# Attention and MoE in one planned stream on one core: a pair's transposes and the next pair's scores taken together, both on half rows of TensorE

## The chip, the cores and the metric

One core of a Trainium2 chip runs the program once. The metric is the device time in microseconds; the figures "before" are three executions, and the profile is of a fourth execution, taken by the hardware profiler. TensorE is written PE here, its weight loads PEld, VectorE DVE, ScalarE ACT, GpSimd POOL, the DMA-issuing engine SP.

## The reference

For 4 batches, 8 heads, 768 positions and 64 values a head, attention looks at the first 8 positions and at the last 96, with a distance bias; its output, 3072 rows of 512 values, goes through a two-matrix MLP with an ELU between:

```python
scores = scale * np.matmul(q, k.transpose(0, 1, 3, 2)) + bias
scores = np.where(is_global | is_local, scores, -1e9)
a = softmax(scores); attn = np.matmul(a, v)
x = attn.transpose(0, 2, 1, 3).reshape(3072, 512)
h = x @ w_in                                  # 512 -> 2048
g = np.where(h > 0, h, np.exp(np.minimum(h, 0)) - 1)
return g @ w_out                              # 2048 -> 512
```

All values are float32. The kernel reaches that precision on TensorE in two ways: with plain f32 operands, or by splitting an operand into a high part of type f32r and a low part that is the rest, and adding the products high x high, low x high and high x low.

## The kernel before, in words

The 3072 rows are cut into 12 groups of 256 rows (4 batches x 3 places in the sequence); a group is two row tiles of 128. The heads are taken in 4 pairs, so a group has 4 pairs of attention and then 16 chunks of the MLP (`moe`, chunks `fc`), each of 12 `h` matmuls of 256 columns (L631) and 6 `o` matmuls of 512 columns (L661). The attention of a group runs while the MLP of the group before it runs, on the same engines.

Nothing in the program text is the order of execution. Every piece of work is added to a `Plan` with its engine and a guessed duration, what it reads and writes, and a due time. `Plan.order` then goes through all of it as a list scheduler: an engine takes, of the pieces whose inputs are ready by the guessed times, the one with the earliest due time. `slack` adds to the time at which inputs from another engine count as ready (`SLACK` 600 ns, `BEHIND` 1200 ns). The order so found is the order in which each engine's instructions are emitted, and on the chip each engine takes them in just that order. Buffers are named slots (`SLOTS`): the PSUM banks are `s0`, `s1` (scores), `t0` (transposes), `v0` (output of attention), `h0`, `h1`, `o0`, `o1` (MLP).

Groups 0 to 3 take attention in plain f32 (`pair32`): there the two heads of a pair lie in partitions 0 to 63 and 64 to 127, and their score matmuls (L532) use 64 rows of the PE array each, with outputs in two banks. From the fifth group on (n = 4 to 11, 32 pairs, 8 of them at the start of a sequence, where the first row tile has 128 keys instead of 232) `pair` and `head` do this for a pair:

- load queries, values and keys (L419, L420) into the single buffers `rqv0` and `rk0`; queries and keys come twice, so that each head has all 128 partitions;
- split queries into `qd` (L445) and `ql` (L450), and keys into `ks` whose upper 64 partitions hold the low part (L287, L295); one matmul of 128 rows then gives two of the three products, and a second with `ql` the third;
- per head and row tile: two score matmuls of 232 columns (L585), the bias and row maximum on DVE (L493), the exponential on ACT (L495); per head one inverse of the sums (L508, L509); per row tile the normalisation on DVE (L481), two transposes on PE of 116 keys each (L599), high part on ACT (L287) and low part on DVE (L295) of the transposed weights, and two matmuls with the values (L611), 256 columns each;
- add the two halves of the output (L287, L472) and split it for the MLP (`xh`, `xl`).

So PE visits attention about twelve times for a pair, with two to four instructions each, and does MLP work between. `build` sets the due times: the pairs of group n are spread evenly over the time from the MLP start of group n-1 to 4000 ns before the MLP start of group n (`LEAD`).

## Time and profile before

| what | us |
|---|---|
| three executions, median (lowest to highest) | 708.03 (706.6 to 709.02) |
| the profiled execution | 704.46 |
| its span, first to last instruction | 702.7 |
| PE busy in the span | 688.3 (98%) |
| PEld / DVE / ACT / POOL busy | 613.1 / 497.7 / 495.1 / 227.0 |
| mean granted clock of PE, share of full | 0.997 |

Busy time of PE counts matmuls from start to a modelled end; matmuls overlap, so a matmul's duration in the trace (283 ns for an `h` matmul) is longer than the distance between the starts of two. Where a row of the timeline joins several matmuls of one kind, its length less the duration of one is the distance between the first and the last start.

### The profile page before, as it was taken

The page shows a single profiled execution, that of the slowest core. Times are in us where ns is not written, and L with a number is a line of the kernel's source. Part 1 is how long each engine was busy: PE and PEld are TensorE (multiplying, and loading weights), DVE is VectorE, ACT ScalarE, POOL GpSimd, SP SyncE. Part 2 cuts the span into 40 slices and gives each one's busy share as a digit, 9 for nine tenths or more (in the row PEclk, how much of TensorE's full clock was granted, in tenths as well). Part 3 has the DMA queues.
Part 4 walks back from the last instruction along what each step waited for, and adds up shares of the span by engine and source line. Part 5 has one row for each costly group of instructions (what it writes and reads, how often), then busy time and mean ns, then how long its engine had stood idle before and what let it go on. Part 6 is the DMA issues. An engine that isn't in the chain of part 4 may idle for free.

```text
span 702.7 us, 13869 instructions
## 1 busy us (share of the span) xinstructions
PE 688.3 (98%) x4707; PEld 613.1 (87%) x4707; DVE 497.7 (71%) x1505; ACT 495.1 (70%) x1442; POOL 227.0 (32%) x306
## 2 busy tenths in 40 slices
PE   8998999999999999999999999999999999999996
PEld 6777888988889989999899999899989998899995
DVE  6998999984467777676667776876687776785211
ACT  5997888764567777767667767677677776766443
POOL 3143001010034434343343453533343344332220
PEclk9999999999999999999999999999999999999998
DMA  7744950002023122212312132223113221310001
GB/s 262 258 148 159 410 205 24 1 21 75 31 91 104 53 59 86 94 53 82 103 54 82 53 104 68 68 83 103 53 53 104 72 62 53 90 45 1 31 1 35
DMA packets 22399, 62.07 MB, mean 88 GB/s; under 512 B 2736, under 2 KB 5040, under 8 KB 22320
## 3 DMA queue, kind: packets, MB, share of 16 engines
q1 hardware_dynamic: 22032, 61.10, 26.5%
q8 instruction: 39, 0.64, 0.4%
q14 instruction: 40, 0.33, 0.1%
q10 hardware_dynamic: 288, 0.00, 0.0%
HBM read 54.80 MB, written 6.29 MB: 87 GB/s over the span
## 4 chain that ended last, share of the span: by engine, by line
PE 87%; DVE 4%; DMA 4%; ACT 2%; issue 1%; POOL 1%; SPq 0%; POOLq 0%; ACTq 0%
PE h L631 35%; PE o L661 35%; PE pv L611 4%; DMA rqv<-in_qkv_dram 4%; PE t L599 4%; PE s L585 3%; PE s L532 2%; PE pv L566 2%; PE t L549 1%; PE none L793 1%; DVE x L472 1%; DVE pr L493 1%; ACT pr L495 0%; DVE ks L295 0%; DVE e L639 0%
## 5 line engine op out<-in xcount | busy, mean ns | idle before, releaser
L631 PEld LDWEIGHTS h<-xh,w 128*128 128x128 f32 x1536 | 223.5, 188 | 23.3 <-issue 0.6
L631 PE MATMUL h<-xh,w 128*128 128x256 f32 x1536 | 243.8, 283 | 0.0
L661 PE MATMUL o<-w,gh 128*128 128x512 f32 x764 | 241.5, 402 | 1.6 <-ACT gh L287 1.6
L295 POOL TENSOR_TENSOR gl<-e,gh 128x256 fp32r<-128x256 f32 x148 | 114.2, 772 | 289.0 <-ACT gh L287 279.2
L661 PE MATMUL o<-w,gl 128*128 128x512 f32 x382 | 147.6, 401 | 0.0
L637 ACT ACTIVATE e<-h 128x256 f32<-128x256 f32 x192 | 73.7, 384 | 102.4 <-PE h L631 97.5
L661 PEld LDWEIGHTS o<-w,gh 128*128 128x128 f32 x764 | 124.1, 189 | 9.9 <-ACT gh L287 3.0
L639 DVE SCALAR_TENSOR_TENSOR e<-e,h 128x256 f32<-128x256 f32 x192 | 80.4, 419 | 66.7 <-ACT e L638 62.6
L631 PE MATMUL h<-xl,w 128*128 128x256 f32 x768 | 122.5, 282 | 0.0
L631 PEld LDWEIGHTS h<-xl,w 128*128 128x128 f32 x768 | 114.3, 188 | 8.2 <-issue 0.6
L287 ACT CAST gh<-e 128x256 fp32r<-128x256 f32 x192 | 77.5, 404 | 45.9 <-DVE e L639 44.7
L493 DVE CUSTOM_DVE_ANT_0 pr<-s,tab 128x232 f32<-128x232 f32 (+1 forms) x192 | 69.0, 377 | 48.9 <-PE s L585 41.3
L495 ACT ACTIVATE pr<-pr,nmax 128x232 f32<-128x232 f32 (+1 forms) x192 | 90.5, 472 | 12.7 <-DVE nmax L493 12.3
L638 ACT ACTIVATE e<-e 128x256 f32<-128x256 f32 x192 | 80.6, 420 | 4.2
L661 PEld LDWEIGHTS o<-w,gl 128*128 128x128 f32 x382 | 70.6, 188 | 2.5 <-issue 0.6
L295 DVE TENSOR_TENSOR pt<-t,pt 116x256 fp32r<-116x256 f32 (+1 forms) x128 | 51.5, 402 | 24.2 <-ACT pt L287 23.5
L481 DVE TENSOR_SCALAR pr<-pr,st 128x232 f32<-128x232 f32 (+1 forms) x144 | 63.7, 476 | 1.2
L472 DVE TENSOR_TENSOR x<-pv,x 64x256 f32<-64x256 f32 x128 | 53.8, 420 | 14.6 <-ACT x L287 11.7
L287 ACT CAST pt<-t 116x256 fp32r<-116x256 f32 (+1 forms) x128 | 45.2, 353 | 7.7 <-PE t L599 7.0
L611 PE MATMUL pv<-pt,vd 116*128 116x256 f32 (+1 forms) x240 | 49.4, 281 | 0.0
L599 PE MATMUL t<-ident,pr 128*116 128x128 f32 (+1 forms) x240 | 47.3, 273 | 1.9 <-DVE pt L295 1.5
L483 POOL TENSOR_SCALAR pr<-pr,st 128x232 f32<-128x232 f32 (+1 forms) x31 | 16.2, 534 | 89.2 <-ACT e L638 36.2
(97 smaller groups left out, 853.4 us busy)
## 6 DMA issues: line engine op xcount, KB each, us to landing
rqv<-in_qkv_dram SPq DMA_DIRECT2D x32, 512.0 KB, 3.9
rk<-in_qkv_dram SPq DMA_DIRECT2D x32, 368.0 KB, 3.1
bits<-in_w_in_dram SPq DMA_DIRECT2D x16, 512.0 KB, 7.0
bits<-in_w_out_dram SPq DMA_DIRECT2D x16, 512.0 KB, 9.5
out_dram<-ob SPq DMA_DIRECT2D x24, 256.0 KB, 2.8
rqv<-in_qkv_dram SPq DMA_DIRECT2D x15, 384.0 KB, 3.4
rk<-in_qkv_dram SPq DMA_DIRECT2D x15, 184.0 KB, 2.8
rqv<-in_qkv_dram SPq DMA_DIRECT2D x1, 192.0 KB, 5.0
```

The source lines that it names most:

```text
L287: self.nc.scalar.copy(out, x)
L295: self.on(e).tensor_tensor(out, x, y, ALU.subtract)
L481: self.nc.vector.tensor_scalar(out, x, sc, None, ALU.mult)
L493: p.add((("DVE", 158 + 1.042 * n, False),), lambda e: nc.vector.tensor_tensor_reduce(pr.t[:, lo:], st_()[:, lo:], tab, -(2.0 ** -(h + 1)), ...
L495: p.add(act(n, extra=200), lambda e: nc.scalar.activation(pr.t[:, lo:], pr.t[:, lo:], AF.Exp, bias=nm, scale=-1.0, accum_out=st.t[:, 0, i: ...
L599: nc.tensor.transpose(tp.t[:kr, a], pr.t[:, blocks[a]], self.ident.t)
L611: nc.tensor.matmul(pv.t[:, i].rearrange("p s w -> p (s w)"), vd.t[:kr, 2 * i + a, j].rearrange("p s d -> p (s d)"), pt.t[:kr, a].rearrange ...
L631: nc.tensor.matmul(h.t, w1.t[:, s, cc * P:(cc + 1) * P], x.t[:, cc], start=n == 0 and cc == 0, stop=n == 2 and cc == self.NCC - 1)
L637: p.add(act(W, True), lambda e: nc.scalar.activation(ex.t, h.t, AF.Relu, scale=-1.0), [h], [ex], d - 8000)
L638: p.add(act(W), lambda e: nc.scalar.activation(ex.t, ex.t, AF.Exp, scale=-1.0), [ex], [ex], d - 8000)
L639: p.add(dve(W), lambda e: nc.vector.scalar_tensor_tensor(ex.t, ex.t, -1.0, h.t, ALU.add, ALU.max), [h, ex], [ex], d - 8000)
L661: nc.tensor.matmul(acc[i].t, g.t[:, i * P:(i + 1) * P], w2.t[:, s], start=fc == f0 and n == 0 and s == HI, stop=fc == f1 - 1 and n == 1)
```

## The change

The split attention of groups 4 to 11 is written anew; groups 0 to 3 and the MLP stay. Queries and keys now lie with one head in each half of the partitions, as in groups 0 to 3; high and low parts are separate tiles `qs`, `ks`. The three products of the scores are matmuls of 64 rows, the two heads side by side, and the transposes take the upper and the lower 64 rows of a weight tile side by side, into two banks (`t0` and `v0`). The transposes of one pair and the scores of the next are emitted as one piece of PE work (`visit`); a last visit holds the transposes of the last pair alone, the first holds scores alone. The matmuls with the values of a pair become one piece per head. Normalised weights have four buffers instead of three, the output of attention may use `t0` as well as `v0`, the sums of a pair share one inverse, the loads are 384 and 184 KB in place of 512 and 368, and the due times of groups 4 on end 8000 ns before the MLP start. The rest of the diff drops `head`, the doubled layout of the inputs and its argument.

```diff
...
+        qs = self.sb("qs", "qs", [P, 2, W], F32R)
+        p.add(act(W), lambda e: nc.scalar.activation(qs.t[:, HI], q32(), AF.Copy, scale=sc), [rqv], [qs], ahead - 4000)
+        p.add(act(KW - k0), lambda e: self.copy(e, ks.t[:, HI, k0:], k32()[:, k0:]), [rk], [ks], ahead - 3900)
+        p.add(dve(W, port=True), lambda e: nc.vector.scalar_tensor_tensor(
+            qs.t[:, LO], q32(), sc, qs.t[:, HI], ALU.mult, ALU.subtract), [rqv, qs], [qs], ahead - 3500)
+        p.add(dve(KW - k0, port=True), lambda e: self.minus(e, ks.t[:, LO, k0:], k32()[:, k0:], ks.t[:, HI, k0:]), [rk, ks], [ks], ahead - 3400)
...
+        ss = [self.bank("s", "s", [P, NT, WN]) for _ in range(2)]
+        prs = [[self.sb("pr", "pr", [P, WN]) for _ in range(NT)] for _ in range(2)]
+        st = self.sb("st", "st", [P, 3, 2 * NT])
+        tiles = [(t0 + i, i * (NG + P)) + self.blocks(t0 + i) for i in range(NT)]
+        def scores():
+            for i, (_, c0, lo, _, _, _) in enumerate(tiles):
+                for x, y in ((HI, HI), (HI, LO), (LO, HI)):
+                    for j in range(2):
+                        r = slice(64 * j, 64 * j + 64)
+                        nc.tensor.matmul(ss[j].t[:, i, lo:], qs.t[r, x, i * P:(i + 1) * P], ks.t[r, y, c0 + lo:c0 + WN],
+                                         start=(x, y) == (HI, HI), stop=x == LO)
+        self.visit(scores, 1.4 * sum(WN - x[2] for x in tiles), [qs, ks], ss, ahead)
         for j in range(2):
-
-            pv = self.bank("pv", "pv", [P, NT, 2, P])
-            self.head(b, 2 * hp + j, t0, j, qd, ql, ks, vd, pv, due + (NT * j - 2 * NT) * step, step)
-            r, o, d = head[j], head[1 - j], due + (NT * j - NT) * step
-            xt = lambda r=r: x.t[r].rearrange("p (i w) -> p i w", i=NT)
-            p.add((("ACT", 385.0, False),), lambda e, r=r, o=o, xt=xt, pv=pv: self.copy(e, xt(), pv.t[o, :, 0]), [pv], [x], d + 500)
-            for s in range(2):
-                p.add(dve(W), lambda e, r=r, s=s, xt=xt, pv=pv: nc.vector.tensor_tensor(xt(), pv.t[r, :, s], xt(), ALU.add),
-                      [pv, x], [x], d + 600 + s)
-        p.add(act(W), lambda e: self.copy(e, xh.t[:, hp], x.t), [x], [xh], due + 700)
-        p.add(pool(W), lambda e: self.minus(e, xl.t[:, hp], x.t, xh.t[:, hp]), [x, xh], [xl], due + 800)
+            for i in range(NT):
+                self.softmax(b, 2 * hp + j, t0 + i, lambda j=j, i=i: ss[j].t[:, i], ss[j], prs[j][i], st, j * NT + i,
+                             ahead + 7000 + (2 * j + i) * step)
+        self.inverse(st, ahead + 4500 + 3 * step)
+        for j in range(2):
+            for i, x in enumerate(tiles):
+                self.norm(prs[j][i], x[2], st, j * NT + i, ahead + 4600 + 3 * step + 2 * j + i, False)
+        tps = [self.bank(c, c, [P, 2 * NT * 2, 64]) for c in ("t", "th")]
+        def transposes():
+            for j in range(2):
+                for i, (_, _, _, a0, kr, blocks) in enumerate(tiles):
+                    for a in range(a0, 2):
+                        for x, tp in enumerate(tps):
+                            r = slice(64 * x, 64 * x + 64)
+                            nc.tensor.transpose(tp.t[:kr, 4 * j + 2 * i + a], prs[j][i].t[r, blocks[a]], self.ident.t[r, r])
+        def rest():
+            pts = [self.sb("pt", "pt", [P, 2 * NT, 2, P], F32R) for _ in range(2)]
+            d = due - 2000
+            for x, tp in enumerate(tps):
+                r = slice(64 * x, 64 * x + 64)
+                for j, pt in enumerate(pts):
+                    if t0:
+                        cut = [(slice(0, HK), slice(0, 4))]
+                    else:
+                        cut = [(slice(0, kr), slice(2 * i + a0, 2 * i + 2)) for i, (_, _, _, a0, kr, _) in enumerate(tiles)]
+                    for rows, c in cut:
+                        n = (c.stop - c.start) * 64
+                        src = lambda j=j, tp=tp, rows=rows, c=c: tp.t[rows, 4 * j + c.start:4 * j + c.stop]
+                        hi = lambda pt=pt, rows=rows, c=c, r=r: pt.t[rows, c, HI, r]
+                        lo = lambda pt=pt, rows=rows, c=c, r=r: pt.t[rows, c, LO, r]
+                        p.add(act(n, True), lambda e, src=src, hi=hi: self.copy(e, hi(), src()), [tp], [pt], d + 2 * x + j)
+                        p.add(dve(n), lambda e, src=src, hi=hi, lo=lo: self.minus(e, lo(), src(), hi()), [tp, pt], [pt], d + 500 + 2 * x + j)
+            self.after = []
+            x = self.sb("x", "x", [P, W])
+            xt = lambda r: x.t[r].rearrange("p (i w) -> p i w", i=NT)
+            head = [slice(0, 64), slice(64, 128)]
+            for j, pt in enumerate(pts):
+                pv = self.bank("pv", "pv", [P, NT, 2, P])
+                def values(e, j=j, pt=pt, pv=pv):
+                    for i, (_, _, _, a0, kr, _) in enumerate(tiles):
+                        for a in range(a0, 2):
+                            nc.tensor.matmul(pv.t[:, i].rearrange("p s w -> p (s w)"), vd.t[:kr, 2 * i + a, j].rearrange("p s d -> p (s d)"),
+                                             pt.t[:kr, 2 * i + a].rearrange("p s w -> p (s w)"), start=a == a0, stop=a == 1)
+                self.after.append(p.add((("PE", 119.0 * sum(2 - x[3] for x in tiles), False),), values, [vd, pt], [pv], due + j, slack=self.BEHIND))
+                r, o = head[j], head[1 - j]
+                p.add((("ACT", 385.0, False),), lambda e, pv=pv, r=r, o=o: self.copy(e, xt(r), pv.t[o, :, 0]), [pv], [x], due + 500 + j)
+                for y in range(2):
+                    p.add(dve(W), lambda e, pv=pv, r=r, y=y: nc.vector.tensor_tensor(xt(r), pv.t[r, :, y], xt(r), ALU.add), [pv, x], [x], due + 600 + 2 * y + j)
+            p.add(act(W), lambda e: self.copy(e, xh.t[:, hp], x.t), [x], [xh], due + 700)
+            p.add(pool(W), lambda e: self.minus(e, xl.t[:, hp], x.t, xh.t[:, hp]), [x, xh], [xl], due + 800)
+        self.prev = transposes, [v for x in prs for v in x], tps, 53.0 * 2 * sum(2 - x[3] for x in tiles), rest
+    def visit(self, scores, cost, reads, ss, due):
+        turn, prs, tps, cost2, rest = self.prev
+        def both(e):
+            turn()
+            scores()
+        self.plan.add((("PE", 330.0 + cost + cost2, False),), both, reads + prs, tps + ss, due, after=self.after, slack=self.BEHIND)
+        rest()
...
+            lead = self.LEAD[n >= self.LATER]
+            lo -= lead[0] if n else 0.0
+            hi -= lead[1] if n else 0.0
...
+                ahead = last - 2500
...
+        todo.append((last + 1, lambda: self.visit(lambda: None, 0.0, [], [], last - 2500)))
...
-    T0, STEP0, STEP, LEAD, NE = 30000.0, 3500.0, 2900.0, (0.0, 4000.0), 3
+    T0, STEP0, STEP, LEAD, NE, LATER = 30000.0, 3500.0, 2900.0, ((0.0, 4000.0), (0.0, 8000.0)), 3, 4
...
-             "s": ["s0", "s1"], "t": ["t0"], "pv": ["v0"], "h": ["h0", "h1"], "o0": ["o0"], "o1": ["o1"],
-             "pr": ["pr0", "pr1", "pr2"], "st": [f"st{i}" for i in range(6)], "pt": ["pt0", "pt1"],
+             "s": ["s0", "s1"], "t": ["t0"], "th": ["v0"], "pv": ["v0", "t0"], "h": ["h0", "h1"], "o0": ["o0"], "o1": ["o1"],
+             "pr": ["pr0", "pr1", "pr2", "pr3"], "st": [f"st{i}" for i in range(6)], "pt": ["pt0", "pt1"],
```

## Rows read from the trace of the kernel before

**Rows 1.** The page, the span and PE's busy time, share and instructions.
```profile
span 702.7 us, 13869 instructions
...
PE 688.3 (98%) x4707; PEld 613.1 (87%) x4707; DVE 497.7 (71%) x1505; ACT 495.1 (70%) x1442; POOL 227.0 (32%) x306
```

**Rows 2.** Busy time of each engine in the stretch from 195 to 655 us, which holds the attention of groups 4 to 11; then granted clock of PE, DMA share and GB/s.
```profile
195.00:655.00 460.00, 458.01 (x3117) 417.31 (x3116) 329.19 (x1008) 330.66 (x988) 185.19 (x227) 1.00 0.23 72
```

**Rows 3.** The page's chain that ended last, shares of the span by engine.
```profile
PE 87%; DVE 4%; DMA 4%; ACT 2%; issue 1%; POOL 1%; SPq 0%; POOLq 0%; ACTq 0%
```

**Rows 4.** Groups of PE's matmuls in the same stretch: line, out<-in, shape, count, busy us, mean ns of one, idle before.
```profile
L631 PE MATMUL h<-xh,w 128*128 128x256 f32 x1060 | 169.9, 284 | 0.0
L661 PE MATMUL o<-w,gh 128*128 128x512 f32 x529 | 169.8, 404 | 0.1
L661 PE MATMUL o<-w,gl 128*128 128x512 f32 x264 | 103.0, 401 | 0.0
L631 PE MATMUL h<-xl,w 128*128 128x256 f32 x528 | 83.9, 281 | 0.0
L611 PE MATMUL pv<-pt,vd 116*128 116x256 f32 (+1 forms) x240 | 49.4, 281 | 0.0
L599 PE MATMUL t<-ident,pr 128*116 128x128 f32 (+1 forms) x240 | 47.3, 273 | 1.9 <-DVE pt L295 1.5
L585 PE MATMUL s<-ks,qd 128*128 128x232 f32 (+1 forms) x128 | 34.3, 279 | 0.0
L585 PE MATMUL s<-ks,ql 128*128 128x232 f32 (+1 forms) x128 | 34.0, 274 | 0.0
```

**Rows 5.** Who waited for whom, in the same stretch, PE's rows (its weight loads carry the waits): us in total, times, longest.
```profile
PEld t L599 <- issue: 2.7, 3, 1.0
...
PEld t L599 <- DVE pt L295: 1.6, 4, 0.6
...
PEld o L661 <- ACT gh L287: 1.2, 6, 0.2
```

**Rows 6.** Timeline of PE: start us, length us, engine, line, out<-in, count. A stretch with MLP matmuls alone, the four score matmuls of a head with what stands around them, and two transposes with what follows.
```profile
378.42 0.63 PE L661 MATMUL o<-w,gh 128*128 128x512 f32 x2
378.88 0.63 PE L631 MATMUL h<-xh,w 128*128 128x256 f32 x4
...
397.05 0.38 PE L599 MATMUL t<-ident,pr 128*116 128x128 f32 x2
397.19 0.71 PE L661 MATMUL o<-w,gh 128*128 128x512 f32 x2
397.74 0.63 PE L631 MATMUL h<-xh,w 128*128 128x256 f32 x4
...
406.58 0.40 PE L611 MATMUL pv<-pt,vd 116*128 116x256 f32 x2
406.81 0.28 PE L585 MATMUL s<-ks,qd 128*128 128x232 f32 x1
...
407.26 0.63 PE L631 MATMUL h<-xh,w 128*128 128x256 f32 x4
```

**Rows 7.** Timeline of PE, the four score matmuls of a head at the start of a sequence (the first and the last of them are shown by the starts of the first and of what follows).
```profile
354.22 0.22 PE L585 MATMUL s<-ks,qd 128*128 128x128 f32 x1
...
354.66 0.64 PE L661 MATMUL o<-w,gh 128*128 128x512 f32 x2
```

**Rows 8.** Timeline of PE and of its weight loads around two visits to half rows in groups 0 to 3 (L532; plain f32, of which each score matmul is recorded twice, so x8 is four matmuls of two passes, the two heads side by side): one at the start of a sequence, whose passes have 128, 128, 232 and 232 columns, and one with 232 columns throughout.
```profile
151.24 0.63 PE L631 MATMUL h<-xl,w 128*128 128x256 f32 x4
151.80 0.89 PE L532 MATMUL s<-rk,rqv 64*128 64x128 f32 x8
152.61 0.51 PE L631 MATMUL h<-xh,w 128*128 128x256 f32 x2
...
151.80 0.52 PEld L532 LDWEIGHTS s<-rk,rqv 64*128 64x128 f32 x8
...
67.06 1.05 PE L532 MATMUL s<-rk,rqv 64*128 64x232 f32 x8
```

**Rows 9.** Timeline of PE and of its weight loads right behind another half-row visit, at the first transposes of full rows: the first load, the two loads after it, and the first two matmuls.
```profile
107.03 0.14 PEld L549 LDWEIGHTS t<-ident,pr 128*128 128x128 f32 x1 [0.29 <-ACT e L637]
...
107.08 0.24 PEld L549 LDWEIGHTS t<-ident,pr 128*116 128x116 f32 x2
...
107.03 0.44 PE L549 MATMUL t<-ident,pr 128*128 128x128 f32 x2
```

**Rows 10.** Groups by form, from 195 to 655 us: what stands between a row tile's scores and its transposes (row maximum on DVE, exponential and its sum on ACT, normalisation on DVE).
```profile
L495 ACT ACTIVATE pr<-pr,nmax 128x232 f32<-128x232 f32 x112 | 54.5, 487 | 4.1 <-DVE nmax L493 3.7
L481 DVE TENSOR_SCALAR pr<-pr,st 128x232 f32<-128x232 f32 x112 | 52.0, 492 | 0.9
...
L493 DVE CUSTOM_DVE_ANT_0 pr<-s,tab 128x232 f32<-128x232 f32 x112 | 43.8, 397 | 39.7 <-PE s L585 34.5 <-PE t L599 4.0
...
L495 ACT ACTIVATION_READ_ACCUMULATOR pr<-pr,nmax 128x1 f32 x128 | 24.2, 189 | 0.0
```

**Rows 11.** The same view, the splitting of queries and keys.
```profile
L450 DVE SCALAR_TENSOR_TENSOR ql<-rqv,qd 128x256 fp32r<-128x256 f32 x64 | 27.8, 443 | 0.2
L445 ACT ACTIVATE qd<-rqv 128x256 fp32r<-128x256 f32 x64 | 26.5, 413 | 2.0 <-DMA rqv<-in_qkv_dram 1.9
...
L295 DVE TENSOR_TENSOR ks<-rk,ks 64x736 fp32r<-64x736 f32 x23 | 24.0, 1045 | 0.7
```

**Rows 12.** The page's DMA issues: KB each, median us from issue to landing.
```profile
rqv<-in_qkv_dram SPq DMA_DIRECT2D x32, 512.0 KB, 3.9
...
rqv<-in_qkv_dram SPq DMA_DIRECT2D x15, 384.0 KB, 3.4
```

More of the change, by code (lines that the diff above doesn't have):

```diff
@@ L33 @@
 KW = NL + NT * (NG + P)
-QC, KC, VC = 2 * W, 2 * KW, 2 * NT * P
+VC = 2 * NT * P
 class Tl:
@@ L392, in weight, with pair @@
         return w
-    def pair(self, b, gi, hp, xh, xl, due, step, X):
+    def pair(self, b, gi, hp, xh, xl, due, ahead, step, X):
         nc, p = self.nc, self.plan
@@ L401, in pair @@
         rows = X.get("rows")
-        rep = 1 if rows else 2
-        nq, nk = rep * W, rep * KW
+        nq, nk = W, KW
         rqv = self.sb("rqv", "rqv", [P, nq + VC], slots=X.get("rqv"))
         rk = self.sb("rk", "rk", [P, nk], slots=X.get("rk"))
-        src = (self.qkv1 if rows else self.qkv)[b, gi, hp]
-        early = due - (9000 if rows else 14000)
+        src = self.qkv[b, gi, hp]
+        early = due - 9000 if rows else ahead - 9000
         if b == gi == hp == 0:
@@ L570, in pair32 @@
             self.held += [o for v in prs[0] + prs[1] + pts for o in v.readers]
-    def head(self, b, h, t0, j, qd, ql, ks, vd, pv, due, step):
-        nc, p, slack, behind = self.nc, self.plan, self.SLACK, self.BEHIND
-        st = self.sb("st", "st", [P, 3, NT])
-        prs = []
-        for i in range(NT):
-            lo = 0 if t0 + i else A0
-            n, c0 = WN - lo, i * (NG + P) + lo
-            s = self.bank("s", "s", [P, WN])
-            prs.append(self.sb("pr", "pr", [P, WN]))
-            def scores(e, i=i, s=s, lo=lo, n=n, c0=c0):
-                for m, x in enumerate((qd, ql)):
-                    nc.tensor.matmul(s.t[:, lo:], x.t[:, j, i * P:(i + 1) * P], ks.t[:, j, c0:c0 + n], start=m == 0, stop=m == 1)
-            p.add((("PE", 130.0 * n / P + 30, False),), scores, [qd, ql, ks], [s], due + i * step - 5000, slack=slack)
-            self.softmax(b, h, t0 + i, lambda s=s: s.t, s, prs[i], st, i, due + i * step)
-        self.inverse(st, due - 3500)
-        for i, pr in enumerate(prs):
-            d = due + i * step
-            lo, a0, kr, blocks = self.blocks(t0 + i)
-            n = (2 - a0) * P
-            self.norm(pr, lo, st, i, d - 3000, False)
-            tp = self.bank("t", "t", [P, 2, P])
-            def transposes(e, pr=pr, tp=tp, a0=a0, kr=kr, blocks=blocks):
-                for a in range(a0, 2):
-                    nc.tensor.transpose(tp.t[:kr, a], pr.t[:, blocks[a]], self.ident.t)
-            p.add((("PE", 75.0 * (2 - a0), False),), transposes, [pr], [tp], d - 2500, slack=behind)
-            pt = self.sb("pt", "pt", [P, 2, 2, P], F32R)
-            p.add(act(n, True), lambda e, pt=pt, tp=tp, a0=a0, kr=kr: self.copy(e, pt.t[:kr, a0:, 0], tp.t[:kr, a0:]), [tp], [pt], d - 2000)
-            p.add(dve(n), lambda e, pt=pt, tp=tp, a0=a0, kr=kr: self.minus(e, pt.t[:kr, a0:, 1], tp.t[:kr, a0:], pt.t[:kr, a0:, 0]),
-                  [tp, pt], [pt], d - 1500)
-            def values(e, pt=pt, a0=a0, i=i, kr=kr):
-                for a in range(a0, 2):
-                    nc.tensor.matmul(pv.t[:, i].rearrange("p s w -> p (s w)"), vd.t[:kr, 2 * i + a, j].rearrange("p s d -> p (s d)"),
-                                     pt.t[:kr, a].rearrange("p s w -> p (s w)"), start=a == a0, stop=a == 1)
-            p.add((("PE", 122.0 * (2 - a0), False),), values, [vd, pt], [pv], d, slack=behind)
@@ L708, in build @@
         todo, self.held, self.parted, self.loads = [], [], [], []
+        self.prev, self.after = ((lambda: None), [], [], 0.0, (lambda: None)), []
+        last = 0.0
         for n, (b, gi) in enumerate(groups):
             lo, hi = (0.0, self.T0) if n == 0 else (start[n - 1], start[n])
-            lo += self.LEAD[0] if n else 0.0
-            hi -= self.LEAD[1] if n else 0.0
+            lead = self.LEAD[n >= self.LATER]
+            lo -= lead[0] if n else 0.0
+            hi -= lead[1] if n else 0.0
             lo, hi = self.ATT.get(n, (lo, hi))
@@ L716, in build @@
                 d = lo + (hp + 1) * (hi - lo) / self.NP
-                todo.append((d, lambda b=b, gi=gi, hp=hp, n=n, d=d, st=st: self.pair(
-                    b, gi, hp, *X[n], d, st, self.EARLY[min(n, len(self.EARLY) - 1)])))
+                X_ = self.EARLY[min(n, len(self.EARLY) - 1)]
+                ahead = last - 2500
+                todo.append((d if X_.get("rows") else last + 1, lambda b=b, gi=gi, hp=hp, n=n, d=d, st=st, X_=X_, ahead=ahead: self.pair(
+                    b, gi, hp, *X[n], d, ahead, st, X_)))
+                last = d
+        todo.append((last + 1, lambda: self.visit(lambda: None, 0.0, [], [], last - 2500)))
         for fc, d in wdue.items():
```

49 lines of the change are left out of this document (16 added, 33 removed).

## The prediction, made before the changed kernel was built or run

> **What bounds the kernel now.** I read the page first: PE is busy 98% of the span [rows 1], and PE makes 87% of the chain that ended last, with no other engine above 4% [rows 3]. Busy time of overlapping matmuls can hide slack, so I then looked at the stretch in which the changed attention lies, 195 to 655 us: PE busy 458.0 of 460 us, at granted clock 1.00, the upper of the two levels (2.4 GHz), while DVE and ACT are busy some 330 us each [rows 2]. The test of whether this is work or waiting is a sum of counts by steps. Steps come from the timeline [rows 6]: two `o` matmuls take 0.46 us from their start to the next start (0.23 each); four `h` matmuls of length 0.63 with 0.28 for the last make (0.63 - 0.28)/3 = 0.117 us each; a head's four score matmuls take 407.26 - 406.81 = 0.45 us, 0.112 each; two transposes 0.38 - 0.27 = 0.11 us apart; two value matmuls 0.40 - 0.28 = 0.12 us apart. With the counts [rows 4]: 1588 x 0.117 + 793 x 0.232 + 256 x 0.112 + 240 x 0.110 + 240 x 0.12 = 185.8 + 184.0 + 28.7 + 26.4 + 28.8 = 453.7 us of 460. So PE's own steps fill the stretch, and about 6 us are waits, of which the view of waits names 5.5 [rows 5]. A microsecond of PE's steps saved here should come off the end; one saved on DVE, ACT, POOL or the DMA queues should not.
>
> **The change part by part.** PE's transposes and scores first. Before, a full pair has 8 transposes and 8 score matmuls: 8 x 0.110 + 8 x 0.112 = 1.776 us. At the start of a sequence there are 6 transposes, and the four scores of a head take 354.66 - 354.22 = 0.44 us [rows 7]: 0.66 + 0.88 = 1.54 us.
>
> After, they are one visit to half rows. Such visits stand in the trace of groups 0 to 3. In the one at 151 us [rows 8] the last `h` matmul starts at 151.24 + 0.63 - 0.28 = 151.59 and ends its step at 151.71; the half-row loads start at 151.80; the second full-row matmul behind starts at 152.61 + 0.51 - 0.28 = 152.84, so the first was under way at 152.72. The visit occupies PE for 1.01 us. Its passes: eight loads in side-by-side pairs within 0.52 - 0.19 = 0.33 us are three steps of 0.11; in the visit at 67 us the last pass starts 1.05 - 0.36 = 0.69 us after the first, which is one exposed load of 0.11 and three steps of 0.194 for 232 columns. Two steps of 0.11 and two of 0.194 are 0.61, so the switch in and out costs 1.01 - 0.61 = 0.40 us: PE runs empty at both edges, and the first load of either side is exposed. The same rows show that the two halves do run side by side, loads and matmuls.
>
> In the new visit the scores are six side-by-side steps (two row tiles by three products). No half-row f32r matmul is in the trace. The bounds are 0.11 us (the load step, and f32r on full rows) and 0.194 (plain f32, the same 232 columns on half rows); I take 0.112, since the full-row step is of the same operand type. At the start of a sequence all six are taken at 0.11; the longer ones could be at 0.194 too.
>
> The transposes are eight side-by-side steps of 64 moving columns. Nor is this form in the trace. A transpose's step is 0.11 for 128 columns [rows 6]; half of that is 0.055. Its load is short: behind another visit the first transpose's load starts at 107.03 and the next load at 107.08, 0.05 to 0.06 us later, and the first matmul step there is 0.44 - 0.27 = 0.17, that is 0.11 and an exposed load of 0.06 [rows 9]. So neither matmul nor load asks for more than 0.055 to 0.06, and I take 0.057; below that I see no reason to go. The upper bound is 0.108, the step of every half-row load that the trace has [rows 8]. Loads of scores behind transposes are exposed by some 0.05, which the shorter exposed load at the visit's start gives back.
>
> By the Trainium skill ("TensorE: Matmul & The Clock Gate", section on LDWEIGHTS) a weight load takes its columns over 1.2 GHz, however few rows it fills, so half rows would save nothing on a load of 116 columns: an estimate of 0.097 us a step from that page, and 2.9 us lost instead of the gain below (710.9). The two loads 0.05 to 0.06 us apart [rows 9] speak against it for transposes; the 0.11 steps of the score loads [rows 8] agree with it.
>
> Sum for PE: a full pair's visit is 0.40 + 8 x 0.057 + 6 x 0.112 = 1.53, so 0.25 us saved, 24 times 5.95. At the start of a sequence 0.40 + 6 x 0.057 + 6 x 0.11 = 1.40, 0.14 saved, 8 times 1.1. There is one visit more than pairs: -0.40. Together 6.7 us less. The value matmuls keep their number and step.
>
> Other engines: the query split is one operation on ACT and one on DVE where there were two of 0.41 and 0.44 us; the low keys are 368 columns instead of 736, about half of 1.05 us [rows 11]; one inverse instead of two. Loads are smaller (384 KB landed in 3.4 us against 3.9 for 512 [rows 12]). All lie beside PE; I count nothing. If DVE became the last to arrive, they would be worth some 1.4 us a pair. The copies of transposed weights keep count and size in full pairs (256 columns), split in two at a sequence start; off the path.
>
> Added waits: a visit waits for four normalised weight tiles, for the banks `t0` and `v0` (read by the last additions of the pair before), for `s0`, `s1` and the next pair's split. Behind a waiting visit stands all of PE's queue, so MLP matmuls too. From a visit's scores to the next visit's transposes the chain is: first row maximum 0.4, four exponentials of 0.49 + 0.19 = 2.7, the inverse 0.4, four normalisations of 0.49 = 2.0: 5.5 us [rows 10], before the MLP's ACT and DVE work gets between. A pair has 460/32 = 14.4 us, and the planner puts nothing on PE before its inputs should be ready, with 1.2 us added. So I cost this at nothing: the MLP's matmuls are the cover. The bounds are the whole present waits gone (-6 us) and, say, a wait of 0.35 us per visit (+11.6). The loads go earlier in due time (from 14,000 before the pair's due time to 9,000 before the visit), but are still held by the single buffer `rqv0`; SP's queue has little else than the output stores. With POOL's two value splits unchanged and 14 us to do it, that stays covered.
>
> The profiled execution, 704.46 us, has a span of 702.7 and 1.8 around it; its forecast is 704.46 - 6.7 = 697.8. It lies 3.6 below the median of the runs shown, so for the median: 708.03 - 6.7 = 701.3.
>
> **The rivals.**
> 1. Half-row transposes step no faster than full-row ones (slower). Place: the eight transpose steps; price: at 0.108 a step, 240 steps x 0.051 = 12.2 us more than I take, 708.0 - 6.7 + 12.2 = 713.6. It decides from 6.7/240 + 0.057 = 0.085 us a step on. For it: every half-row load step in the trace is 0.11. Against: the transposes' own loads [rows 9].
> 2. Half-row f32r scores stream at 0.194 as plain f32 does: 24 x 6 + 8 x 3 steps x 0.082 = 13.8 us more, 715.1. Against it: the operand type sets the step on full rows.
> 3. Visits wait. One piece now hangs on four tiles, two banks and a split; at 0.35 us each 33 visits take 11.6, 712.9; at 0.15, 706.3, no change to be told. From 0.20 us each the gain is gone. For it: almost all present waits of PE's loads are at transposes [rows 5]. Against: the 14.4 us.
> 4. More gain: with a visit per pair in place of some twelve, half of the 6 us of waits goes: 698.3.
>
> **How the numbers follow.** My forecast 58%; more gain 10%; waits that cancel it 9%; rival 1 12%; rival 2 3%; waits that make it slower 8%. A measurement of this kernel tells about 0.3% (2.1 us) from no change. So faster 0.68, within it 0.09, slower 0.23. The likeliest case alone has 699 to 704.5 (a transpose step of 0.055 to 0.07, runs 1.2 us apart). The range for 8 in 10 reaches from somewhat below rival 4 to rival 1: 696.5 to 713.5.
>
> **What would show it.** In the profile after: transposes of 64 columns in side-by-side pairs with starts 0.055 to 0.06 us apart from pair to pair (0.1 is rival 1); half-row scores 0.11 apart (0.19 is rival 2); an edge of 0.09 us before a visit; a visit of 1.5 us on PE; waits of PE for DVE `pr` or `x` summing to no more than some 5 us (over 10 is rival 3); ACT and DVE with about 25 and 40 us less work and no effect of it. The prediction is wrong if the sum of steps falls as reckoned and the span does not, or if a visit lasts over 1.78 us.

## The result, and the profile after

The changed kernel takes 695.65 us (694.88 to 696.93) against 707.32 us of the kernel before in the same job: ratio 0.9833, 95% interval 0.9807 to 0.9859. In three later jobs the same pair gave 0.9878 (0.9848 to 0.9907), 0.9851 (0.9836 to 0.9866) and 0.9864 (0.9837 to 0.9890). The forecast, 701.3 us or 0.9905, had the sign right and the size too small: 11.7 us were gained where 6.7 were foretold, and the time lies 0.85 us under the range.

The page after, span and busy time of the engines:

```profile
span 695.2 us, 14518 instructions
...
PE 682.3 (98%) x5075; PEld 600.7 (86%) x5075; DVE 459.1 (66%) x1442; ACT 474.5 (68%) x1445; POOL 217.9 (31%) x302
```

Busy time from 195 to 655 us, as [rows 2] for the kernel before; the columns are the same:

```profile
195.00:655.00 460.00, 459.28 (x3544) 411.74 (x3543) 291.67 (x949) 314.81 (x996) 179.92 (x229) 1.00 0.17 51
```

PE is still what bounds the kernel, at the same granted clock of 1.00; DVE lost 37 us of work in the stretch and ACT 16 (reckoned: 40 and 25); whether this counted is taken up with the run on full rows. PE's weight loads waited, after, in the same stretch, for:

```profile
PEld t L483 <- PE h L644: 3.5, 14, 0.3
PEld t L483 <- issue: 3.4, 13, 0.4
PEld o L674 <- ACT gh L287: 2.2, 5, 0.7
```

Beside [rows 5], the waits of up to 1.0 us before transposes are gone; the new rows are short ones, 27 of about 0.25 us, at the first loads of visits, most of them the edge that every visit has.

One visit in the timeline of PE (start us, length us); of the transposes' steps the first three and the last are shown:

```profile
211.40 0.39 PE L674 MATMUL o<-w,gl 128*128 128x512 f32 x1
211.72 0.27 PE L483 MATMUL t<-ident,pr 64*116 64x64 f32 x1
211.72 0.27 PE L483 MATMUL th<-ident,pr 64*116 64x64 f32 x1
211.83 0.22 PE L483 MATMUL t<-ident,pr 64*116 64x64 f32 x1
211.83 0.22 PE L483 MATMUL th<-ident,pr 64*116 64x64 f32 x1
211.88 0.22 PE L483 MATMUL t<-ident,pr 64*116 64x64 f32 x1
...
212.17 0.22 PE L483 MATMUL t<-ident,pr 64*116 64x64 f32 x1
212.17 0.22 PE L483 MATMUL th<-ident,pr 64*116 64x64 f32 x1
212.20 0.91 PE L463 MATMUL s<-ks,qs 64*128 64x232 f32 x12
213.04 0.73 PE L674 MATMUL o<-w,gh 128*128 128x512 f32 x2
```

The two halves start together; from the second step to the eighth there are 0.34 us, 0.057 each. The `o` matmul ahead ends its step at 211.40 + 0.235 = 211.635, the second `o` matmul behind starts at 213.04 + 0.73 - 0.39 = 213.38 and so the first was under way at 213.38 - 0.235 = 213.145: the visit takes 1.51 us, forecast 1.53. Those at a sequence start take 1.41, forecast 1.40. By the starts of the single matmuls in the trace, which the view joins, the scores are 0.112 us apart from their second step to their sixth.

To see where the time went, the trace of each run was cut by PE's own work, not by the clock: from the 565th `h` matmul, ahead of which every run has the same number of matmuls of each kind, to the 2113th, the first of the last group's MLP. Within it, each unbroken run of transposes and scores was timed from the end of the step ahead of it to the start of the step behind (steps of 0.117 for `h`, 0.235 for `o`, 0.120 for `pv`); the rest is MLP and value matmuls. The kernel before has 198 such runs, about six a pair, the changed kernel 33. All in us:

```
run                     begins  length   transposes   rest   tail
                                         and scores
before                   197.8   451.2      60.4     390.8   53.6
r1_before                197.9   451.0      60.0     391.1   53.5
after                    199.8   441.9      49.6     392.3   53.4
r2_after                 201.9   442.0      49.7     392.3   53.3
r5_after                 198.1   442.0      49.7     392.4   53.4
r9_after                 199.1   442.0      49.6     392.4   53.4
r3_apart                 201.6   450.8      59.7     391.1   53.5
r4_full_t                200.0   451.2      60.1     391.1   53.5
r6_early                 199.3   441.7      49.8     391.9   53.6
r7_early_turn            199.3   441.9      50.0     391.9   53.7
r8_full_rows             199.5   446.1      54.9     391.2   53.8
r10_later                198.9   444.7      48.0     396.7   53.5
r11_before_later         199.0   468.0      60.2     407.8   52.3
r12_lead4                198.9   450.9      48.7     402.2   52.9
r13_before_lead8         198.9   449.8      59.0     390.8   53.7
```

The stretch is the same in every profiled execution of a kernel to 0.2 us, and the change takes 9.3 us from it. What differs between executions is when it begins: the changed kernel's four profiles have 198.1 to 201.9. In these four the begin goes with PE's granted clock from 20 to 60 us: 1.00 in r5_after and r9_after (198.1 and 199.1), 0.96 in the first profile (199.8), 0.91 in r2_after (201.9); 1.00 is the upper of its two levels (2.4 GHz) throughout, the others are means over both. Columns as [rows 2], r5_after and r2_after:

```profile
20.00:60.00 40.00, 36.47 (x300) 28.20 (x298) 38.34 (x129) 36.62 (x113) 11.99 (x18) 1.00 0.57 187
20.00:60.00 40.00, 36.62 (x271) 27.54 (x268) 35.12 (x117) 34.02 (x104) 10.90 (x18) 0.91 0.53 174
```

Both profiles of the kernel before have 1.00 there. Its own spread is not explained by the clock: at one mean granted clock of 0.998 it took 703.94 and 708.97 us in the job of r9_after. Both profiles of the kernel before are of executions (704.46 and 704.2 us) 3.6 and 1.7 us under the medians shown with them, and the changed kernel's first profile is of one (696.93) 1.3 us above its own, so the two first profiles are only 7.5 us apart and the medians 11.7.

The expectations below were written with a mark 12 `h` matmuls later (their "third MLP group" counts from 0). By it the stretch of the kernel before is 448.3 and 447.8, that of the changed one 438.1 or 438.2 in all four profiles; but the first visit, 1.06 us of scores alone, lies ahead of that mark in the changed kernel, so by it the gain looks 0.9 us larger than it is. Measured values are quoted by the table.

### The profile page after: what moved, and what is told of

It is laid out like the page before. It is cut to its first block, busy times and chain, and to the rows that moved or that the text cites. A ratio compares the mean times of both kernels' runs of the same rounds, so it can differ in the third digit from the quotient of the medians.

```text
span 695.2 us, 14518 instructions
## 1 busy us (share of the span) xinstructions
PE 682.3 (98%) x5075; PEld 600.7 (86%) x5075; DVE 459.1 (66%) x1442; ACT 474.5 (68%) x1445; POOL 217.9 (31%) x302
## 4 chain that ended last, share of the span: by engine, by line
PE 85%; ACT 5%; DVE 4%; DMA 3%; issue 1%; POOL 1%; SPq 0%; DVEq 0%; POOLq 0%; ACTq 0%
PE o L674 36%; PE h L644 35%; PE pv L512 4%; PE s L463 3%; PE t L483 2%; DMA rqv<-in_qkv_dram 2%; PE s L591 1%; ACT pr L554 1%; PE t L608 1%; PE pv L625 1%; DMA bits<-in_w_out_dram 1%; DVE pr L540 1%; PE none L813 1%; DVE e L652 1%; DVE x L519 1%
## 5 line engine op out<-in xcount | busy, mean ns | idle before, releaser
L644 PEld LDWEIGHTS h<-xh,w 128*128 128x128 f32 x1536 | 228.9, 188 | 28.5 <-issue 1.1
L295 POOL TENSOR_TENSOR gl<-e,gh 128x256 fp32r<-128x256 f32 x145 | 108.5, 748 | 312.6 <-ACT gh L287 312.6
L674 PEld LDWEIGHTS o<-w,gh 128*128 128x128 f32 x764 | 127.5, 189 | 15.6 <-ACT gh L287 4.0
L554 ACT ACTIVATE pr<-pr,nmax 128x232 f32<-128x232 f32 (+1 forms) x192 | 92.2, 481 | 9.1 <-DVE nmax L552 9.1
L552 DVE CUSTOM_DVE_ANT_0 pr<-s,tab 128x232 f32<-128x232 f32 (+1 forms) x192 | 66.1, 374 | 9.9 <-PE s L463 6.9
L295 POOL TENSOR_TENSOR vd<-rqv,vd 128x512 fp32r<-128x512 f32 (+1 forms) x32 | 39.5, 1234 | 2.4
L554 ACT ACTIVATION_READ_ACCUMULATOR pr<-pr,nmax 128x1 f32 x192 | 38.4, 200 | 0.0
L512 PEld LDWEIGHTS pv<-pt,vd 116*128 116x128 f32 (+1 forms) x240 | 33.8, 190 | 2.4
L512 PE MATMUL pv<-pt,vd 116*128 116x256 f32 (+1 forms) x240 | 35.5, 282 | 0.0
```

What stands on the lines that cost most here:

```text
L295: self.on(e).tensor_tensor(out, x, y, ALU.subtract)
L512: nc.tensor.matmul(pv.t[:, i].rearrange("p s w -> p (s w)"), vd.t[:kr, 2 * i + a, j].rearrange("p s d -> p (s d)"), pt.t[:kr, 2 * i + a].r ...
L552: p.add((("DVE", 158 + 1.042 * n, False),), lambda e: nc.vector.tensor_tensor_reduce(pr.t[:, lo:], st_()[:, lo:], tab, -(2.0 ** -(h + 1)), ...
L554: p.add(act(n, extra=200), lambda e: nc.scalar.activation(pr.t[:, lo:], pr.t[:, lo:], AF.Exp, bias=nm, scale=-1.0, accum_out=st.t[:, 0, i: ...
L644: nc.tensor.matmul(h.t, w1.t[:, s, cc * P:(cc + 1) * P], x.t[:, cc], start=n == 0 and cc == 0, stop=n == 2 and cc == self.NCC - 1)
L674: nc.tensor.matmul(acc[i].t, g.t[:, i * P:(i + 1) * P], w2.t[:, s], start=fc == f0 and n == 0 and s == HI, stop=fc == f1 - 1 and n == 1)
```

## The experiments

**Both kernels once more.** No edit.

> The kernel before once more, unchanged, for a second profile of it. Theory A (the profile of before that the prediction used was an early stage that went quickly, and the stretch of split attention is the same in every execution): from the first h matmul of the third MLP group to the first of the last, 448 us again within 0.5, the split attention's transposes and scores 60 us again, and the 2 to 4 us by which the timed runs lie above that profile stand ahead of 200 us. Theory B (the surplus is waits at the loads of the split attention, which differ from execution to execution): the stretch is 450 us or more and the time ahead of 200 us as it was.

> The changed kernel once more, unchanged. Theory A: the stretch from the first h matmul of the third MLP group to the first of the last is 438 us again within 0.5, with seven visits of 1.76 us and the rest at 1.50 or 1.40; the time ahead of it differs by some us from the first profile's 203.7. Theory B: the stretch itself differs by over 1 us.

Measured: 705.88 us against 705.64 in the same job, and 697.77. By the mark of the expectations 447.8 and 438.1, transposes and scores 60.0, and again seven visits of 1.76 us. The stretch is as fixed as theory A said, and the begin of the changed kernel moved from 199.8 to 201.9. That the timed runs of the kernel before owe their surplus to the time ahead of 200 us was not seen directly, since this profile too fell in a quick execution.

**The visit cut in two.** One full-row matmul between transposes and scores, in the 31 visits that have both.

```diff
+                nc.tensor.matmul(ss[0].t[:, 0, A0:A0 + 64], qs.t[:, HI, :P], ks.t[:, HI, A0:A0 + 64], start=True, stop=True)
             for i, (_, c0, lo, _, _, _) in enumerate(tiles):
                 for x, y in ((HI, HI), (HI, LO), (LO, HI)):
```

> The changed kernel with one full-row matmul of 64 columns between a visit's transposes and its scores, so that PE leaves half rows and comes back; nothing else differs, in the order neither. Theory (each switch in and out costs 0.40 us, as the half-row visits of before show): 31 visits have it, a visit grows by 0.38 to 0.42 us (0.40 for the switch, 0.03 for the matmul, less the 0.05 by which the scores' loads were exposed anyway), the time by 12 to 13 us over the changed kernel, which is at or above the kernel before. Rival (PE can load across the change, and the edges seen before came from waits): under 0.15 us a visit, less than 5 us.

Measured: 706.19 us, 8.4 above the changed kernel in that job and equal to the kernel before (ratio 1.0, 0.9984 to 1.0017). In its timeline of PE, from a last transpose to what follows the visit:

```profile
213.97 0.22 PE L485 MATMUL th<-ident,pr 64*116 64x64 f32 x1
214.12 0.30 PE L460 MATMUL s<-ks,qs 128*128 128x64 f32 x1
214.35 0.93 PE L465 MATMUL s<-ks,qs 64*128 64x232 f32 x12
215.21 0.74 PE L679 MATMUL o<-w,gh 128*128 128x512 f32 x2
```

From the last transpose to the first score there are 0.38 us where the changed kernel has 0.03. A visit grew by 0.37 us (1.51 to 1.88, and 1.41 to 1.78), just under the lower bound given, and transposes and scores together by 10.1 us. The time grew by less than 12, since the seven long visits of the changed kernel became less long (1.94 where 1.76 and 0.37 make 2.13) and 1.2 us of the rest went. The switch is real and costs what the old visits had shown.

**Transposes on full rows.** The banks' shape and the reads of the copies behind them follow; the core of the edit:

```diff
-                        for x, tp in enumerate(tps):
-                            r = slice(64 * x, 64 * x + 64)
-                            nc.tensor.transpose(tp.t[:kr, 4 * j + 2 * i + a], prs[j][i].t[r, blocks[a]], self.ident.t[r, r])
+                        nc.tensor.transpose(tps[j].t[:kr, 2 * i + a], prs[j][i].t[:, blocks[a]], self.ident.t)
```

> The changed kernel with its transposes on full rows (eight of 128 columns, one bank per head), scores on half rows as changed; copies behind them of the same count and size. Theory (half rows save the transposes' moving columns: eight steps of 0.11 instead of eight of 0.057): a full visit 0.40 us longer, one at a sequence start 0.29, together 24 x 0.40 + 8 x 0.29 = 12 us more than the changed kernel, so the transposes alone carry all of the gain in steps. Rival (the gain is from fewer and larger visits, with fewer waits): under 4 us more.

Measured: 705.65 us, 7.9 above the changed kernel, again the time of the kernel before (0.9992, 0.9977 to 1.0006). Its timeline of PE:

```profile
211.80 0.60 PE L481 MATMUL t<-ident,pr 128*116 128x128 f32 x4
212.24 0.60 PE L481 MATMUL th<-ident,pr 128*116 128x128 f32 x4
212.77 0.93 PE L463 MATMUL s<-ks,qs 64*128 64x232 f32 x12
213.63 0.73 PE L673 MATMUL o<-w,gh 128*128 128x512 f32 x2
```

Four transposes are (0.60 - 0.27)/3 = 0.11 apart. A full visit takes 1.93 us (0.42 more), one at a sequence start 1.72 (0.31 more), as expected; no visit has the extra 0.25 us any more. So without half-row transposes nothing is left of the gain in steps, and half-row scores alone are a loss: transposes and scores last 60.1 us here and 54.9 in r8_full_rows below, which has everything on full rows. By the steps the scores save 8 x 0.112 - 6 x 0.112 = 0.22 us in a full visit and the transposes 0.42, against one switch of 0.40 for both. Half-row transposes with full-row scores were not run.

**Three runs of one job: the changed kernel, the old slot lists for groups 0 to 3, and a new order of the two banks.**

```diff
-             {"rqv": ["rqv0", "ks0"], "rk": ["rk0", "qs0"], "pr": ["pr0", "pr1", "pr2", "pr3"], "rows": True}, {}]
+             {"rqv": ["rqv0", "ks0"], "rk": ["rk0", "qs0", "ql0"], "pr": ["pr0", "pr1", "pr2", "x3"], "rows": True}, {}]
```

(`pr3` is named `x3` in the other two lists too, and a slot `ql0` is declared), then on top of it (the cut line behind takes bank and rows by `x`):

```diff
-                        for x, tp in enumerate(tps):
+                        for x in ((1, 0) if held and held[1].slot == tps[1].slot else (0, 1)):
```

> The changed kernel unchanged, on the chip and in the job of the next three, for their comparison. All theories: the stretch from the first h matmul of the third MLP group to the first of the last is 438.1 us again; it begins between 203 and 206 us.

> The changed kernel with the fourth buffer of the weights under the name that the fourth slot had before (in the planner's tie-break it sorts behind the slots of the MLP weights again) and with a third slot for the keys of group 3 as before; so PE's order is that of the kernel before up to about 130 us. Theory (the changed kernel's stretch begins 3 to 5 us later than before's because the planner, by those two slot lists, orders groups 0 to 3 differently; nothing of half rows is in it): the stretch begins at 200.5 to 202 us, the time is 3 to 4 us under the changed kernel's. Rival (the late start is the chip's, of the loads at the start): the beginning is at 203 to 206 as before, and the time the same within 1 us.

> The kernel with the early slot lists as before, and besides, each visit's first transpose goes to the bank whose reader finished last. Theory (seven of the full visits last 1.76 instead of 1.51 us because the second transpose's bank was released later than the first's, and needs a wait of its own between the first and second load, in an empty PE): no visit over 1.55 us, the stretch of the split attention 1.5 to 2 us shorter than in the kernel with the early lists alone. Rival (the 0.25 us is the fetch of instructions or another thing at that place): visits of 1.76 remain, five or more.

Measured: 696.35, 698.02 and 697.57 us. The old lists do give PE the old order up to the 317th `h` matmul, but the stretch begins at 199.3 us, within the changed kernel's own 198.1 to 201.9, and the time is not better. That theory fell: what moves the begin is not shown to be the slot lists. The new order of banks fell too: seven visits of 1.80 to 1.84 us remain. In the timeline of all engines of r5_after, around such a visit:

```profile
220.59 0.39 PE L674 MATMUL o<-w,gl 128*128 128x512 f32 x1
220.64 0.43 DVE L519 TENSOR_TENSOR x<-pv,x 64x256 f32<-64x256 f32 x1
...
220.91 0.13 PEld L483 LDWEIGHTS t<-ident,pr 64*116 64x116 f32 x1 [0.24 <-issue]
...
221.18 0.13 PEld L483 LDWEIGHTS th<-ident,pr 64*116 64x116 f32 x1
```

The visit's first load goes out at 220.91, the second 0.27 us later instead of at once. In between, at 221.07, DVE ends the last addition of the pair before, which reads the bank that the second transpose is to write. In all seven long visits of this run the second load follows the end of that addition by 0.11 to 0.12 us. It is a wait for DVE, so taking the banks in another order only moves it ahead of the first load.

**Everything on full rows, in one visit.**

```diff
-                for x, y in ((HI, HI), (HI, LO), (LO, HI)):
-                    for j in range(2):
-                        r = slice(64 * j, 64 * j + 64)
-                        nc.tensor.matmul(ss[j].t[:, i, lo:], qs.t[r, x, i * P:(i + 1) * P], ks.t[r, y, c0 + lo:c0 + WN],
-                                         start=(x, y) == (HI, HI), stop=x == LO)
+                for j in range(2):
+                    for x in range(2):
+                        nc.tensor.matmul(ss[j].t[:, i, lo:], qs.t[:, x, i * P:(i + 1) * P], ks.t[:, x, c0 + lo:c0 + WN], start=x == 0, stop=x == 1)
```

(on top of the full-row transposes above). The scores of both heads are summed by this, so that the output is not the reference's; the run is for its time alone.

> The changed kernel with neither transposes nor scores on half rows: a visit has eight transposes of 128 columns and eight score matmuls of 128 rows, two products each, as many as the kernel before had, but all in one place. The scores are not the reference's (both heads are summed), only the work of PE is that of before. Theory (grouping takes away the waits at the single transpose bank and the small visits' extra, some 4 us; half rows take away 6.7): transposes and scores last 24 x 1.78 + 8 x 1.54 = 55 us, the stretch 444.5 to 446 us, that is 3 us under before's 448 and 7 above the changed kernel's 438.1. Rival (the whole 10 us are from half rows): 448. Rival (they are from grouping): 441 or less.

Measured: 700.06 us, ratio to the kernel before 0.9893 (0.9878 to 0.9908). Its visit in the timeline of PE, and all that its weight loads waited for from 195 to 655 us:

```profile
211.13 0.60 PE L479 MATMUL t<-ident,pr 128*116 128x128 f32 x4
211.57 0.60 PE L479 MATMUL th<-ident,pr 128*116 128x128 f32 x4
211.92 1.14 PE L462 MATMUL s<-ks,qs 128*128 128x232 f32 x8
212.89 0.64 PE L671 MATMUL o<-w,gh 128*128 128x512 f32 x2
```

```profile
PEld o L671 <- ACT gh L287: 0.9, 3, 0.5
```

Transposes and scores take 54.9 us, which is the sum of steps that the prediction made for the kernel before (24 x 1.776 + 8 x 1.54 = 54.9); there they take 60.4. So all of the change but the half rows, with as many matmuls of the same size on PE, is worth 5.1 us of the stretch (451.2 to 446.1), and the half rows 4.1 more (to 442.0).

Which part of it did that, this run doesn't tell: beside the grouping it has the second transpose bank, the earlier due times and the lighter work of DVE. The trace of the kernel before shows where the 5.5 us lay. Of its 198 runs, 14 last over 0.15 us longer than their steps, 5.0 us together. Seven of these are transposes (3.2 us), whose load goes out 0.05 to 0.12 us after DVE ended a low-part subtraction, which reads the one bank of transposes; by this the three waits that [rows 5] call "issue" were for DVE too. In four of the seven (2.1 us) the subtraction began 0.03 to 0.04 us after DVE ended a split of keys of 1.3 to 1.46 us:

```profile
443.46 1.46 DVE L295 TENSOR_TENSOR ks<-rk,ks 64x736 fp32r<-64x736 f32 x1
...
444.96 0.42 DVE L295 TENSOR_TENSOR pt<-t,pt 116x256 fp32r<-116x256 f32 x1
...
445.50 0.19 PEld L599 LDWEIGHTS t<-ident,pr 128*116 128x116 f32 x2 [1.04 <-issue]
```

In the changed kernel that split takes 0.54 us on average instead of 1.05. So the halved split of keys is a rival to the grouping for the longest of these waits, and no run keeps the one without the other. The other seven of the 14 are scores, two of them with transposes ahead, 0.26 or 0.27 us each; their cause was not read.

**More slack.** First a visit's slack, then, in the kernel before, that of transposes and value matmuls:

```diff
-        self.plan.add((("PE", 330.0 + cost + cost2, False),), both, reads + prs, tps + ss, due, after=self.after, slack=self.BEHIND)
+        self.plan.add((("PE", 330.0 + cost + cost2, False),), both, reads + prs, tps + ss, due, after=self.after, slack=2 * self.BEHIND)
```

```diff
-    SLACK, BEHIND = 600.0, 1200.0
+    SLACK, BEHIND = 600.0, 2400.0
```

> The changed kernel unchanged, for comparison with the next in the same job. Stretch from the first h matmul of the third MLP group to the first of the last: 438.1 us once more, seven visits of some 1.76 us.

> The changed kernel with the planner's slack of a visit at 2400 ns instead of 1200 (inputs from other engines count as ready 1.2 us later, freed banks 0.36 us later), so that MLP matmuls go ahead of it. Theory (the 0.25 us of seven visits is a wait for the last addition of the pair before, on DVE, which reads the bank that the transposes want and ends 0.1 us after the visit began): no full visit over 1.55 us, transposes and scores 46.9 us instead of 48.6, the stretch 436.3 to 437 us, the time 1 to 2 us under the changed kernel's. Rival (it is no wait for another engine): visits of 1.76 remain and the stretch is 438 or more.

> The kernel before with the planner's slack BEHIND at 2400 ns instead of 1200 for transposes and value matmuls, nothing else. Theory (some 3 us of before's stretch are waits of transposes for the single bank's low-part subtraction on DVE, which the planner takes to be done too early): transposes alone lose their waits (none over 0.35 us for a pair of two), the stretch is 445 us instead of 448, the time 2 to 3 us under before's, with no half rows and no grouping. Rival (those waits only go elsewhere, since a later transpose makes the softmax and the values late): 447.5 or more.

Measured: 696.77, 698.59 and 721.43 us. In r10_later no visit lasts over 1.53 us and transposes and scores fall to 48.0 us: what the seven visits had on top was that wait. But the rest rose by 4.3 us. The weight loads of r10_later waited, in the same stretch, for

```profile
PEld o L674 <- ACT gh L287: 5.4, 9, 1.2
...
PEld h L644 <- ACT xh L287: 1.2, 1, 1.2
```

the first 2.2 us in the changed kernel. So the MLP waits at these two places; that later visits push their softmaxes between the MLP's operations on ACT and DVE is my reading, not traced. The expectation was right on the visit and wrong on the time. In r11_before_later it is the same on a larger scale: 17 us lost in the stretch, most of it before `h`:

```profile
PEld h L631 <- ACT xh L287: 11.9, 7, 2.7
PEld h L631 <- DVE e L639: 2.7, 5, 0.6
```

The MLP of a group waits for the attention of that group, which came too late. The rival that I had written beside it, that such waits go elsewhere, is what holds; I had not thought of a price of this size.

**The due times alone.** The changed kernel with the old ones, and the kernel before with the new ones:

```diff
-    T0, STEP0, STEP, LEAD, NE, LATER = 30000.0, 3500.0, 2900.0, ((0.0, 4000.0), (0.0, 8000.0)), 3, 4
+    T0, STEP0, STEP, LEAD, NE, LATER = 30000.0, 3500.0, 2900.0, ((0.0, 4000.0), (0.0, 4000.0)), 3, 4
```

```diff
-            hi -= self.LEAD[1] if n else 0.0
+            hi -= (8000.0 if n >= 4 else self.LEAD[1]) if n else 0.0
```

> The changed kernel with the due times of groups 4 on ending 4000 ns before the MLP start, as in the kernel before, in place of 8000. Theory (a pair's output now comes one visit later than its scores, and without the earlier due times the MLP's h matmuls wait for xh at the start of a group): waits of h for xh of 1 to 3 us at each of eight groups, the stretch 446 to 460 us instead of 438.1, visits themselves 1.40 to 1.77 as before. Rival (the order follows readiness and not due times, so that the lead does nothing): 438 to 439.

> The kernel before with the due times of groups 4 on ending 8000 ns before the MLP start in place of 4000, nothing else. Theory (the waits of before hang on the single transpose bank, so earlier due times don't take them away): transposes and scores again 59 to 61 us, the stretch 447 to 449. Rival (the earlier due times are what takes the waits away): 444 or less.

Measured: 704.5 and 704.1 us against 705.76 of the kernel before. With the old due times the changed kernel loses nearly all of its gain: transposes and scores take 48.7 us, and the rest 402.2, that is 9.9 more. Its weight loads waited for

```profile
PEld o L674 <- ACT gh L287: 8.5, 11, 1.4
...
PEld h L644 <- DVE e L652: 2.4, 3, 1.1
```

so the loss is of the size expected, at another place than I had said: not `h` for `xh` at the start of groups, but `o` for `gh` and `h` for the ELU within them. In the kernel before the new due times bring 1.4 us of stretch, and most of the waits at the transposes stay:

```profile
PEld t L599 <- issue: 5.5, 6, 1.0
```

Five of these six waits, 1.0 us each, stand again right behind a split of keys of 1.46 us on DVE and the subtraction that follows it. The due times are needed for the gain and don't make it.

No version here beats the changed kernel by more than its executions differ.

## Why the prediction was wrong, point by point

- **What bounds the kernel.** Right: PE before and after. But the 37 us less of DVE's work and the 10 MB less of loads were not tested by themselves; that DVE's work counts for nothing beside PE is not shown (see the waits).
- **PE's steps.** Right to 0.3 us. Forecast: 54.9 us of transposes and scores before, 48.2 after, 6.7 saved. Measured without waits: 54.9 (r8_full_rows) and 48.0 (r10_later), 6.9. The transposes' 0.057 us, taken from half a full-row step and the 0.05 to 0.06 us between two loads [rows 6, 9], holds; so rival 1 falls. By the Trainium skill ("TensorE: Matmul & The Clock Gate", section on LDWEIGHTS) a load of 116 columns would make the step 0.097, an estimate from that page. The visit at 211 us, 0.057 a step with load and matmul, disagrees for transposes. The half-row f32r scores go at the full-row pace, 0.112 a step, so rival 2 falls too. The switch of 0.40 us was read from two visits [rows 8]; taking the visit in two showed 0.37.
- **Waits: here the prediction failed.** I wrote "So I cost this at nothing" of the waits, with their whole going, 6 us, as the bound, and gave "more gain", half of that, 10%. The 6 us that the sum of steps left over [rows 2, 4] were not a background that stays, but lay almost wholly at the transposes and scores of the kernel before: these last 60.4 us where their steps make 54.9, and with all of the change but the half rows they last 54.9. So 5.5 us went there. With it fails "All lie beside PE; I count nothing" of the other engines' work, as far as the trace goes: 3.2 of the 5.5 us were transposes that waited for DVE. Whether grouping, the second bank or the shorter split of keys took the waits away stays open; the due times alone bring 1.4 us (r13_before_lead8). Back came 1.6 us at the seven visits that wait for DVE's last addition, and 1.5 us in the rest, where the waits of `o` for `gh` rose from 1.2 to 2.2: 60.4 - 49.6 = 10.8 saved, 1.5 lost, 9.3 in sum instead of 6.7.
- **The other 2.4 us** of the medians' 11.7 are not in the stretch (9.3) nor in the tail (0.2): by that they should lie ahead of it, where the begin wanders by some 4 us from execution to execution, but no profile shows it. In the four jobs the medians are 11.7, 7.9, 10.8 and 10.3 us apart. That the stretch begins later or earlier for a cause in the change is not shown. With the stretch's gain alone the time would have been 707.3 - 9.3 = 698.0 us, inside the range; so it is partly chance that the time fell below it, as it did in one of the three later jobs (697.77, 696.35 and 696.77 us). The failure of the step on the waits doesn't hang on that: it is read from the stretch.
- **Rival 3, waits at visits.** The place was right and the price small: seven of 33 visits wait 0.25 us, 1.6 us of the 11.6 that I gave as the bound. What I did not see is that the cover, MLP work in front of the visit, has a price of its own: r10_later bought those 1.6 us with 4.3 elsewhere, and r12_lead4 shows 9.9 us of such waits one due time away. The due times, a line of the change that the prediction mentioned for the loads alone, decide whether there is a gain.

## What to carry to other kernels

When the sum of an engine's steps leaves a remainder, price the remainder too: find in the trace which pieces of work it hangs on and what another engine did just before them, ask whether the change leaves both standing, and put its whole going into the forecast's range. Half rows cost a fixed switch in and out (0.37 to 0.40 us here), so gather in one visit what gains from them: the f32 transposes (0.057 against 0.11 us a step, 0.42 us a full visit) only just pay for the switch, and the scores (six steps instead of eight, 0.22 us) pay only by riding along. In this planned order, waits that were planned away came back at other work (r10_later, r11_before_later); change due times together with the grouping, and measure both.

## What the runs showed of the hardware that was not expected

A wait within a half-row visit was not hidden by the loads behind it: DVE's addition was late by 0.16 us after the first load (220.91 to 221.07), and the visit lasted 0.25 us longer than its fellows. Transposes of 64 f32 columns with 116-column loads go side by side at 0.057 us a step, so from the second step to the eighth two weight loads and two matmuls went out every 0.057 us.
